# Gate weights turned by TensorE transposes instead of an element-wise copy, and a new order of scores and values in sigmoid attention ahead of two mixture layers

## The chip, the cores and the metric

The kernel runs on one core of one Trainium2 chip. The metric is the device time of one execution in microseconds. The kernel before was timed three times: 807.14, 807.19 and 807.71 us, a median of 807.19 us. Lower is better.

## What is computed

Three steps in fp32: attention with a sigmoid in place of the softmax (4 batches, 12 heads, 448 positions, head size 64), a layer that takes the larger of three projections and projects the result again, and a mixture of eight experts of which each token takes one.

```python
scores = scale * np.matmul(q, k.transpose(0, 1, 3, 2)) - np.log(S)
attn = 1.0 / (1.0 + np.exp(-scores))
x = np.matmul(attn, v)                      # -> [1792, 768]
h = np.maximum(np.maximum(x @ w1, x @ w2), x @ w3)
x = h @ w_out
logits = x @ w_gate + modality_bias[modality_id]     # w_gate is [768, 8]
e_idx = np.argmax(logits, axis=1)
...
for e in range(E):
    h = np.maximum(x[mask] @ w1[e], 0.0)
    out[mask] = gate_w[mask, None] * (h @ w2[e])
```

## The kernel before

The change lies in the first stage, attention. Its unit of work is a pair of heads of one batch: 24 units, numbered u, handled two at a time in a loop over j (A = 2j, B = 2j + 1). The 448 keys of a unit are three blocks of 128 and a rest of 64. For each unit there are four kinds of TensorE work:

- `emit_qk` (line 295): scores of the three full blocks of keys, six matmuls for each block, fp32r operands, rows 0 to 63 of the array for one head and 64 to 127 for the other. Query and key are first split by VectorE into a rounded part and a rest (`split_qk`, lines 275 and 276, into the tile `kq`, one buffer for even units and one for odd), and the product is made of three terms.
- `emit_qk_last` (line 310): scores of the last 64 keys of both units of a pair at once, four fp32 matmuls, one on each quarter of the array, straight from the loaded input.
- `emit_av` (line 320): attention times values over the three full blocks, six fp32 matmuls, columns 0 to 63 for one head and 64 to 127 for the other, into the PSUM tile `X` (tag `x0` for even units, `x1` for odd).
- `emit_av_last` (line 328): the same for the last 64 keys of both units, four fp32 matmuls on quarters of the array.

Each fp32 matmul shows in the trace as two records. Scores go into PSUM tiles `s` of which three exist (tags `a0`, `a1`, `t`); ScalarE takes the sigmoid from there (line 285), one instruction for each block and one for the last keys of a pair: seven for each pair of units. When the last keys are added, VectorE takes `X` out of PSUM (`evac_X`, lines 336 and 337).

The order on TensorE, ScalarE, VectorE and SyncE is the order in which the code is written; GpSimd is ordered by the framework. All loads of this stage are issued on SyncE, in that order, and each DMA there waits for the DMA issued eight before it. Inputs are loaded two pairs ahead: in pair j, after `emit_qk_last(j)`, units 2j + 4 and 2j + 5 (`load_qk`, line 254, into the tiles `u`; `load_v`, lines 260 to 265). The load of query and key waits for the scores that still read its buffer. In pair 4, after these loads, four small transfers stand on the same queue:

```python
nc.sync.dma_start(out=slots.rearrange("(p c) o -> p (c o)", p=128), in_=idx)
with nc.allow_non_contiguous_dma(reason="small"):
    nc.sync.dma_start(out=wgT, in_=w_gate.rearrange("d e -> e d"))
nc.sync.dma_start(out=mb, in_=m_bias.partition_broadcast(128))
nc.sync.dma_start(out=midi, in_=mid.bitcast(I32).rearrange("(i p t) -> p i t", p=128, t=2))
```

`wgT` is a scratch tensor in DRAM that holds the gate weights with the experts as rows; it is read in the second stage (line 436), one expert's row at a time, spread over the partitions. From pair 2 on, `background(2.5, ...)` gives VectorE some 2.5 us of another job in each pair: weights of the second stage, loaded as 64-bit numbers (`stage`, line 216), are turned into fp32 (lines 165 to 182). The second stage begins with the matmuls of line 457 as soon as the last `X` is out.

Of the kernel before, what the change touches and what calls it, by code (L numbers as in the profile page):

```python
# [28 lines left out]
def attn_moe_kernel(  # L29
# [15 lines left out]
    nc = tc.nc  # L45
    B, HP, D, _, _, S = qk.shape
    NT, DM = out.shape
    E, _, FF = ew1.shape
    KB = DM // 128
    FB = FF // 128  # L50
    NU = B * HP
# [23 lines left out]
    def hold(tag, name, *shape):  # L75
        return pool.tile([128, *shape], F32, tag=tag, name=name)

    def r(ap):
        return ap.bitcast(F32R)

    def cut(a, off, *shape):

        n = 1
        for s in shape:
            n *= s
        a = a[:, off:off + n]
        if len(shape) == 2:
            a = a.rearrange("p (a b) -> p a b", a=shape[0])
        elif len(shape) == 3:
            a = a.rearrange("p (a b c) -> p a b c", a=shape[0], b=shape[1])  # L90
        return a
# [10 lines left out]
    NW = 2 * NJ  # L102
# [5 lines left out]
    kq = [cut(kq_, 4 * S * i, 2, 2, S) for i in range(2)]  # L108
    u1, u2, u3 = (hold(f"U{i}", f"u{i}", 2048) for i in range(3))
    qk_in = [cut(u, 2 * S * i, 2, S) for u in (u1, u2) for i in range(2)]  # L110
    v4 = hold("K1", "v4", 2, NW + 1, D)
    v_in = [cut(u3, (NW + 1) * D * i, NW + 1, D) for i in range(4)] + [v4[:, i] for i in range(2)]

    stage = [hold(f"S{i}", f"stage{i}", KB * 256).bitcast(I32) for i in range(2)]
# [7 lines left out]
    wgT = dram.tile([E, DM], F32, name="wgT")  # L122
# [3 lines left out]
    ident = cpool.tile([128, 128], F32, name="ident")  # L126
# [21 lines left out]
    def ps(tag, shape, name):  # L148
        return psum.tile(shape, F32, tag=tag, name=name)
# [101 lines left out]
    def load_qk(u):  # L251
        b, hp = divmod(u, HP)
        for h in range(2):
            nc.sync.dma_start(out=qk_in[u % 4][D * h:D * (h + 1)], in_=qk[b, hp, :, h])  # L254
# [12 lines left out]
    def split_qk(u):  # L267
        src, kt = qk_in[u % 4], kq[u % 2]
        if u == 0:
            nc.vector.tensor_copy(out=r(kt[:, 0, 0]), in_=src[:, 0])  # L270
            nc.scalar.activation(out=r(kt[:, 0, 1]), in_=src[:, 1], func=ACTF.Copy)
            for i in range(2):
                nc.vector.tensor_tensor(out=r(kt[:, 1, i]), in0=src[:, i], in1=kt[:, 0, i], op=ALU.subtract)
        else:
            nc.vector.tensor_copy(out=r(kt[:, 0]), in_=src)  # L275
            nc.vector.tensor_tensor(out=r(kt[:, 1]), in0=src, in1=kt[:, 0], op=ALU.subtract)
# [3 lines left out]
    def scores():  # L280
        s_n[0] += 1
        return ps(("a0", "a1", "t")[s_n[0] % 3], [128, 2, 512], "s")

    def sigmoid(dst, s):
        nc.scalar.activation(out=dst, in_=s[:, :, 0:S], func=ACTF.Sigmoid, scale=qscale, bias=nlns)  # L285

    def emit_qk(u):

        kt = kq[u % 2]
        for g in range(NJ):  # L290
            s = scores()
            for n, (a, x) in enumerate(((0, 0), (0, 1), (1, 0))):
                for h in range(2):
                    p = slice(D * h, D * (h + 1))
                    nc.tensor.matmul(s[:, h, 0:S], r(kt[p, a, 0, 128 * g:128 * (g + 1)]), r(kt[p, x, 1]),  # L295
                                     start=(n == 0), stop=(n == 2))
            sigmoid(atb[u % 2][:, 2 * g:2 * g + 2], s)

    def quarter(i, h):

        return slice(SR * (h ^ i), SR * ((h ^ i) + 1))

    def emit_qk_last(j):

        s = scores()
        for i in range(2):
            src = qk_in[(2 * j + i) % 4]
            for h in range(2):
                p = slice(D * h, D * (h + 1))
                nc.tensor.matmul(s[quarter(i, h), i, 0:S], src[p, 0, 128 * NJ:], src[p, 1], start=True, stop=True)  # L310
        sigmoid(atl[j % 2], s)
# [3 lines left out]
    def emit_av(u):  # L315
        X_t[u] = ps(f"x{u % 2}", [128, 512], "X")
        vt, at = v_in[u % 6], atb[u % 2]
        for g in range(NJ):
            for h in range(2):
                nc.tensor.matmul(X_t[u][64 * h:64 * h + 64, 0:S], vt[:, 2 * g + h], at[:, 2 * g + h],  # L320
                                 start=(g == 0), stop=False)

    def emit_av_last(j):
        for i in range(2):
            u = 2 * j + i
            for h in range(2):
                p = quarter(i, h)
                nc.tensor.matmul(X_t[u][64 * h:64 * h + 64, 0:S], v_in[u % 6][p, NW], atl[j % 2][p, i],  # L328
                                 start=False, stop=True)

    def evac_X(u):
        b, hp = divmod(u, HP)
        src = X_t.pop(u)[:, 0:S]
        dR = xR[hp][:, b * S:(b + 1) * S]
        dL = xL[hp][:, b * S:(b + 1) * S]
        nc.vector.tensor_copy(out=r(dR), in_=src)
        nc.vector.tensor_tensor(out=r(dL), in0=src, in1=dR, op=ALU.subtract)

    with tc.manual_schedule(engines={mybir.EngineType.PE, mybir.EngineType.Activation, mybir.EngineType.DVE, SP}):
        load_qk(0)  # L340
        nc.vector.memset(gw, 0.0)
        nc.vector.memset(ones, 1.0)
        make_identity(nc, ident)
# [35 lines left out]
        for j in range(NU // 2 + 1):  # L379
            A, B, more = 2 * j, 2 * j + 1, j < NU // 2  # L380
            if more:
                emit_qk(A)
            if j:
                emit_av(B - 2)
                emit_av_last(j - 1)
                evac_X(A - 2)
                evac_X(B - 2)
            if not more:
                break
            emit_qk_last(j)  # L390
            for u in (A + 4, B + 4):
                if u < NU:
                    load_qk(u)
                    load_v(u)
            if A + 2 < NU:
                split_qk(A + 2)
            if j == 1:
                load_chunk()
            if j == 4:
                nc.sync.dma_start(out=slots.rearrange("(p c) o -> p (c o)", p=128), in_=idx)  # L400
                with nc.allow_non_contiguous_dma(reason="small"):
                    nc.sync.dma_start(out=wgT, in_=w_gate.rearrange("d e -> e d"))
                nc.sync.dma_start(out=mb, in_=m_bias.partition_broadcast(128))  # L403
                nc.sync.dma_start(out=midi, in_=mid.bitcast(I32).rearrange("(i p t) -> p i t", p=128, t=2))
            if j >= 2:
                background(2.5, stop=(1, 0))
            emit_qk(B)
            emit_av(A)
            if B + 2 < NU:
                split_qk(B + 2)  # L410
        background(99, stop=(1, 0))

        nc.vector.tensor_copy(out=midf, in_=midi[:, :, 0])
# [488 lines left out]
        for p, (i, n) in enumerate(todo[:NF * NCH]):  # L902
# [9 lines left out]
            else:  # L912
                f = n - 2 * KB
# [27 lines left out]
        d = xo[xo_n[0] % 3]  # L941
# [7 lines left out]
    with tc.For_i(NSTAT, nreg, 1) as iv:  # L949
        nc.sync.dma_start(out=idx2, in_=slots.rearrange("(p c) o -> p (c o)", p=128)[:, bass.ds(iv * 2, 2)])  # L950
        nc.sync.dma_start(out=e_dyn, in_=exd[0:1, bass.ds(iv, 1)])
        e = nc.values_load(e_dyn[0:1, 0:1], engines=(SP,), min_val=0, max_val=E - 1)
# [51 lines left out]
```

## Time and profile before

| | before |
|---|---|
| median of 3 runs | 807.19 us |
| the profiled execution | 807.75 us |
| its span, first to last instruction | 806.0 us |
| mean granted TensorE clock | 0.974 of 2.4 GHz |
| TensorE busy with matmuls | 760.3 us, 94% of the span |
| VectorE busy | 448.5 us, 56% |
| ScalarE busy | 258.6 us, 32% |
| attention, until the first matmul of line 457 | 168.63 us |

The profiled execution is one execution, 0.07% above the median. Its time is 1.75 us longer than its span, which is what lies around the first and the last instruction. Busy time of TensorE is the time covered by matmul records; TensorE works nearly the whole span, so what ends the kernel is read from the chain of waits: followed back from the last instruction, it is on TensorE for 87% of the span and on SyncE's DMA queue for 6%. In the chain, the waits and the timeline a line number is that of the kernel, `SPq` is SyncE issuing a DMA, and `out<-in` names the tiles. `PEclk` is the granted clock as a share of 2.4 GHz.

### The profile page before, as it was taken

The numbers are of one execution on the slowest core, as the hardware profiler recorded it, in microseconds if no ns is written. First come the engines' busy times: TensorE is split into PE (matmuls) and PEld (weight loads), VectorE is DVE, ScalarE is ACT, GpSimd is POOL, SyncE is SP. The second block draws the span as 40 slices with busy tenths as digits, with TensorE's granted clock in tenths as the row PEclk, the third lists the DMA queues.
The fourth block names the chain that finished last, engine by engine and source line by source line (L and its number), as shares of the span: only waits on it lengthen the run. The fifth ranks groups of instructions, "written<-read, shape, count | busy, mean of one in ns | idle before, by whom it ended". The sixth has DMA issues, their size and how long they took to land.

```text
span 806.0 us, 11821 instructions
## 1 busy us (share of the span) xinstructions
PE 760.3 (94%) x4698; PEld 642.0 (80%) x4698; DVE 448.5 (56%) x751; ACT 258.6 (32%) x362; POOL 65.2 (8%) x82
## 2 busy tenths in 40 slices
PE   9998059999999999999999999999999999999994
PEld 5454034479999999999997888998999999899993
DVE  3685047666696878784305822246665466555532
ACT  5665025520101010010003323245544445454522
POOL 0000000000000000000010060230220302021000
PEclk9999569999999999999999999999999999999998
DMA  8767596313242131220000196343657401064000
GB/s 206 206 148 2 3 225 164 109 40 118 77 153 83 59 117 59 79 79 1 0 1 1 54 368 243 102 144 133 249 171 263 157 22 59 14 246 148 20 25 18
DMA packets 50920, 88.04 MB, mean 109 GB/s; under 512 B 14219, under 2 KB 32908, under 8 KB 50862
## 3 DMA queue, kind: packets, MB, share of 16 engines
q1 hardware_dynamic: 47294, 75.71, 33.1%
q0 software_dynamic: 3568, 11.54, 4.3%
q8 instruction: 39, 0.64, 0.3%
q14 instruction: 19, 0.16, 0.1%
HBM read 94.95 MB, written 11.57 MB: 132 GB/s over the span
## 4 chain that ended last, share of the span: by engine, by line
PE 87%; SPq 6%; issue 2%; DMA 2%; DVE 1%; POOL 0%; ACT 0%; POOLq 0%; DVEq 0%
PE acc L457 33%; PE oacc L796 15%; PE hacc L775 14%; PE acc L523 7%; PE X L320 6%; PE s L295 5%; SPq L403 4%; PE acc2b L523 4%; DMA u<-in_qk_dram 2%; PE X L328 1%; PE xT L736 1%; PE s L310 1%; SPq L254 1%; PE lgp L483 1%; SPq L216 1%
## 5 line engine op out<-in xcount | busy, mean ns | idle before, releaser
L457 PE MATMUL acc<-xR,w_ring 128*128 128x448 f32 x864 | 210.5, 365 | 0.0
L457 PEld LDWEIGHTS acc<-xR,w_ring 128*128 128x128 f32 x864 | 162.2, 188 | 13.5 <-issue 0.7
L796 PE MATMUL oacc<-wo_ck,xh 128*128 128x512 f32 (+1 forms) x672 | 124.0, 340 | 0.0
L775 PE MATMUL hacc<-xh,wo_ck 128*128 128x256 f32 x1008 | 122.3, 283 | 0.0
L775 PEld LDWEIGHTS hacc<-xh,wo_ck 128*128 128x128 f32 x1008 | 121.9, 192 | 0.3
L796 PEld LDWEIGHTS oacc<-wo_ck,xh 128*128 128x128 f32 x672 | 102.8, 188 | 13.8
L285 ACT ACTIVATE at<-s,nlns 128x896 f32<-128x896 f32 x84 | 78.2, 1008 | 80.8 <-PE s L295 51.3
L457 PE MATMUL acc<-xLa,w_ring 128*128 128x448 f32 x360 | 102.2, 365 | 0.0
L295 PE MATMUL s<-kq 64*128 64x448 f32 x432 | 53.7, 388 | 31.8 <-DVE kq L275 31.2
L295 PEld LDWEIGHTS s<-kq 64*128 64x128 f32 x432 | 38.8, 190 | 54.2 <-issue 39.7
L182 DVE TENSOR_TENSOR wo_ck<-raw,wo_ck 128x512 fp32r<-128x512 f32 (+1 forms) x108 | 75.4, 743 | 6.0 <-ACT wo_ck L181 5.8
L523 PE MATMUL acc<-wo_ck,hs 128*128 128x512 f32 x252 | 77.4, 394 | 0.0
L457 PEld LDWEIGHTS acc<-xLa,w_ring 128*128 128x128 f32 x360 | 67.6, 188 | 5.3
L181 ACT ACTIVATE wo_ck<-raw 128x512 fp32r<-128x512 f32 (+1 forms) x108 | 67.0, 671 | 11.5 <-PE hacc L775 11.3
L523 PEld LDWEIGHTS acc<-wo_ck,hs 128*128 128x128 f32 x252 | 47.2, 188 | 11.4 <-ACT wo_ck L181 0.8
L523 PE MATMUL acc2b<-wo_ck,hs 128*128 128x256 f32 x252 | 56.2, 280 | 0.0
L439 DVE SCALAR_TENSOR_TENSOR gk<-wof,gk 128x768 f32<-128x768 f32 x48 | 45.9, 956 | 1.2
L461 ACT ACTIVATE hA<-acc 128x896 f32<-128x896 f32 x8 | 7.4, 920 | 115.1 <-PE acc L457 115.1
L782 DVE SCALAR_TENSOR_TENSOR xh<-hacc,xh 128x1024 fp32r<-128x1024 f32 x14 | 17.1, 1224 | 46.3 <-ACT xh L781 46.3
L727 POOL DMA_INDIRECT xg<-x2d,idx x30 | 30.0, 1000 | 148.2 <-PE xT L736 101.0
L523 PEld LDWEIGHTS acc2b<-wo_ck,hs 128*128 128x128 f32 x252 | 41.5, 189 | 0.1
L320 PE MATMUL X<-at,u 128*64 128x448 f32 x192 | 40.4, 557 | 0.0
(175 smaller groups left out, 666.5 us busy)
## 6 DMA issues: line engine op xcount, KB each, us to landing
raw<-in_moe_w_dram SPq DMA_DIRECT2D x24, 1024.0 KB
stage<-in_moe_w_dram SPq DMA_DIRECT2D x18, 768.0 KB
u<-in_qk_dram SPq DMA_DIRECT2D x48, 224.0 KB
raw<-in_moe_w_dram SPq DMA_DIRECT2D x12, 768.0 KB
raw_S<-in_moe_w_dram SPq DMA_DIRECT2D x12, 768.0 KB
stage<-in_moe_w_out_dram SPq DMA_DIRECT2D x6, 768.0 KB
x2d<-xo SPq DMA_DIRECT2D x14, 256.0 KB
gk<-wgT SPq DMA_DIRECT2D x8, 384.0 KB
```

The source lines that it names most:

```text
L181: nc.scalar.activation(out=r(dR), in_=src, func=ACTF.Copy)
L182: nc.vector.tensor_tensor(out=r(dL), in0=src, in1=dR, op=ALU.subtract)
L285: nc.scalar.activation(out=dst, in_=s[:, :, 0:S], func=ACTF.Sigmoid, scale=qscale, bias=nlns)
L295: nc.tensor.matmul(s[:, h, 0:S], r(kt[p, a, 0, 128 * g:128 * (g + 1)]), r(kt[p, x, 1]), start=(n == 0), stop=(n == 2))
L320: nc.tensor.matmul(X_t[u][64 * h:64 * h + 64, 0:S], vt[:, 2 * g + h], at[:, 2 * g + h], start=(g == 0), stop=False)
L403: nc.sync.dma_start(out=mb, in_=m_bias.partition_broadcast(128))
L439: nc.vector.scalar_tensor_tensor(out=junk, in0=wof[kb], scalar=1.0, in1=wgb[e % 2], op0=ALU.mult, op1=ALU.mult, accum_out=gw[:, kb, e:e + 1])
L457: nc.tensor.matmul(acc[:, c, 0:S], r(m[:, a, kk, :]), r(x[kk][:, c0 + S * c:c0 + S * (c + 1)]), start=(kk == 0 and n == 0), stop=(kk == KB ...
L523: nc.tensor.matmul(acc_t[t, c], r(hs[t][:, a, kk, :]), r(wo_rl[c][:, kk, b]), start=(kk == 0 and n == 0), stop=(kk == KB - 1 and n == 2))
L727: nc.gpsimd.indirect_dma_start(out=xg[i % 2][s][:, XC[c][0]:XC[c][1]], out_offset=None, in_=x2d[c], in_offset=bass.IndirectOffsetOnAxis(ap ...
L775: nc.tensor.matmul(acc[:, f], r(w[a][:, 128 * f:128 * (f + 1)]), r(x[:, kk]), start=(kk == 0 and m == 0 and f % 2 == 0), stop=(kk == KB - ...
L796: nc.tensor.matmul(dst, r(x[:, f, 128 * s:128 * (s + 1)]), r(w[a][:, c0:c1]), start=(f == 0 and m == 0 and not (shared and s == 1)), stop= ...
```

## The change

- The transfer into `wgT` on SyncE is gone. Instead GpSimd loads `w_gate` as it is, 128 partitions by 6 rows of 8 numbers, at the very start of the kernel, ahead of its other work, into a part of the tile that also holds two of the six value buffers (tag K1).
- In pair 0, between the scores of the last keys and the scores of unit B, six TensorE transposes turn it (`turn_gate`) into two PSUM tiles of tags `x0` and `x1`, VectorE copies them out, and GpSimd stores the turned weights to `wgT`.
- `emit_av(B)` moves from the next pair, where it stood after `emit_qk(A)`, to the end of its own pair, behind `emit_av(A)`. So the values of the two units stand in one run, and `emit_av_last(j - 1)` and `emit_qk_last(j)` stand between `emit_qk(A)` and `emit_qk(B)`.
- `split_qk(B + 2)` moves ahead of `background(2.5, ...)` and of the values.

```diff
-    v4 = hold("K1", "v4", 2, NW + 1, D)
+    k1 = hold("K1", "k1", 3 * DM)
+    v4 = cut(k1, 0, 2, NW + 1, D)
+    wg_in = cut(k1, 2 * (NW + 1) * D, KB, E)
+    wg_t = k1[0:E, 2 * DM:3 * DM]
...
+    def turn_gate():
+
+        for x, k0, k1 in ((0, 0, 4), (1, 4, KB)):
+            T = ps(f"x{x}", [128, 512], "wgp")
+            for k in range(k0, k1):
+                nc.tensor.transpose(T[0:E, 128 * (k - k0):128 * (k - k0 + 1)], wg_in[:, k], ident)
+            nc.vector.tensor_copy(out=wg_t[:, 128 * k0:128 * k1], in_=T[0:E, 0:128 * (k1 - k0)])
+        nc.gpsimd.dma_start(out=wgT, in_=wg_t)
...
         load_qk(0)
+        nc.gpsimd.dma_start(out=wg_in, in_=w_gate.rearrange("(k p) e -> p k e", p=128))
         nc.vector.memset(gw, 0.0)
...
             if more:
                 emit_qk(A)
             if j:
-                emit_av(B - 2)
                 emit_av_last(j - 1)
                 evac_X(A - 2)
                 evac_X(B - 2)
             if not more:
                 break
             emit_qk_last(j)
+            if not j:
+                turn_gate()
             for u in (A + 4, B + 4):
...
             if j == 4:
                 nc.sync.dma_start(out=slots.rearrange("(p c) o -> p (c o)", p=128), in_=idx)
-                with nc.allow_non_contiguous_dma(reason="small"):
-                    nc.sync.dma_start(out=wgT, in_=w_gate.rearrange("d e -> e d"))
                 nc.sync.dma_start(out=mb, in_=m_bias.partition_broadcast(128))
                 nc.sync.dma_start(out=midi, in_=mid.bitcast(I32).rearrange("(i p t) -> p i t", p=128, t=2))
+            emit_qk(B)
+            if B + 2 < NU:
+                split_qk(B + 2)
             if j >= 2:
                 background(2.5, stop=(1, 0))
-            emit_qk(B)
             emit_av(A)
-            if B + 2 < NU:
-                split_qk(B + 2)
+            emit_av(B)
         background(99, stop=(1, 0))
```

SyncE's queue in pair 4, from the last load of that pair (`v`) to the first of pair 5 (`qk`). `6144x1x1` is 6144 pieces of one number. Before:

```order
L265 DMA u_73<-in_v_dram 64x64 x2
L400 DMA slots<-idx 128x30
L402 DMA wgT<-in_moe_w_gate_dram 6144x1x1
L403 DMA mb<-in_moe_modality_bias_dram 128x16
L404 DMA midi<-in_moe_modality_id_dram 128x14x2
L216 DMA stage_75<-in_moe_w_dram 128x6x256
L254 DMA u_72<-in_qk_dram 64x896 x2
```

Changed:

```order
L268 DMA u_73<-in_v_dram 64x64 x2
L414 DMA slots<-idx 128x30
L415 DMA mb<-in_moe_modality_bias_dram 128x16
L416 DMA midi<-in_moe_modality_id_dram 128x14x2
L219 DMA stage_75<-in_moe_w_dram 128x6x256
L257 DMA u_72<-in_qk_dram 64x896 x2
```

One row has left; the transfer of the modality numbers (`midi`) and all that follows keep their places.

TensorE from the first scores to the scores of unit 3 (`s<-kq x18` is one unit's scores, `s<-u` the last keys' scores, `X<-at,u x6` one unit's values, `X<-at,u x4` the last keys' values). Before:

```order
L295 MATMUL s<-kq 128x448 x18
L310 MATMUL s<-u_71 64x448 x4
L295 MATMUL s<-kq 128x448 x18
L320 MATMUL X<-at,u_73 64x448 x6
L295 MATMUL s<-kq 128x448 x18
L320 MATMUL X<-at,u_73 64x448 x6
L328 MATMUL X<-at,u_73 64x448 x4
L310 MATMUL s<-u_72 64x448 x4
L295 MATMUL s<-kq 128x448 x18
```

Changed:

```order
L298 MATMUL s<-kq 128x448 x18
L313 MATMUL s<-u_71 64x448 x4
L339 MATMUL wgp<-ident,k_74 8x128 x6
L298 MATMUL s<-kq 128x448 x18
L323 MATMUL X<-at,u_73 64x448 x12
L298 MATMUL s<-kq 128x448 x18
L331 MATMUL X<-at,u_73 64x448 x4
L313 MATMUL s<-u_72 64x448 x4
L298 MATMUL s<-kq 128x448 x18
```

The six transposes (`wgp`) have come in, and the second run of six value matmuls has moved up to the first, so that the last keys' values and scores follow the scores of unit 2 directly.

## Rows read from the trace of the kernel before

**Rows 1.** The page: its span, and lines of the span in 40 equal slices (busy tenths of TensorE, its granted clock in tenths, busy tenths of the DMA engines).

```profile
span 806.0 us, 11821 instructions
PE   9998059999999999999999999999999999999994
PEclk9999569999999999999999999999999999999998
```

**Rows 2.** The chain of waits in order of time, one pair of units (start us, us, what).

```profile
35.83 2.02 PE s L295 x14
37.84 2.41 PE X L320 x12
40.25 0.91 PE X L328 x8
41.17 0.75 PE s L310 x8
41.92 2.09 PE s L295 x18
44.00 2.41 PE X L320 x12
```

**Rows 3.** The same chain at the end of attention.

```profile
163.06 4.66 PE X L320 x24
...
168.63 1.42 PE acc L457 x6
```

**Rows 4.** The same chain from 58.95 us on.

```profile
58.95 30.48 SPq L403
...
89.47 0.43 SPq L404
...
89.95 4.43 SPq L216
...
94.50 5.39 SPq L254
...
99.98 8.59 DMA u<-in_qk_dram
...
108.59 0.64 DVE kq L275
...
110.40 3.35 PE s L295 x16
113.76 3.24 PE X L320 x12
```

**Rows 5.** Waits between 70 and 115 us (engine, line, for whom: us in total, times, longest).

```profile
DVE kq L275 <- DMA u<-in_qk_dram: 33.2, 1, 33.2
...
PE s L295 <- DVE kq L275: 31.2, 1, 31.2
```

**Rows 6.** The timeline of 50 to 125 us (start us, us, engine, line; in brackets the idle time before and what ended it).

```profile
52.51 1.10 SPq L254 DMA_DIRECT2D u<-in_qk_dram  x2
52.64 3.71 ACT L285 ACTIVATE at<-s,nlns 128x896 f32<-128x896 f32 x4 [2.52 <-PE s L310]
...
58.09 0.81 SPq L402 DMA_DIRECT2D wgT<-in_moe_w_gate_dram  x1
...
109.37 0.74 PE L295 MATMUL s<-kq 64*128 64x448 f32 x2 [31.22 <-DVE kq L275]
```

**Rows 7.** Busy time in stretches: from:to, its length, busy us of TensorE (matmuls, weight loads), VectorE, ScalarE, GpSimd, each with its instructions, the granted clock, the busy share of the DMA engines, and GB/s.

```profile
59.00:78.00 19.00, 19.00 (x134) 8.71 (x134) 12.22 (x18) 11.90 (x13) 0.00 (x0) 1.00 0.72 10
...
89.40:94.40 5.00, 0.00 (x0) 0.00 (x0) 0.00 (x0) 0.00 (x0) 0.00 (x0) 0.50 0.15 1
...
108.60:114.00 5.40, 4.34 (x20) 3.11 (x22) 5.23 (x8) 2.15 (x3) 0.00 (x0) 0.50 1.07 216
114.00:168.60 54.60, 54.60 (x383) 25.47 (x379) 34.17 (x49) 30.61 (x33) 0.00 (x0) 0.99 0.50 132
```

**Rows 8.** The same view of the start.

```profile
3.00:4.00 1.00, 1.00 (x4) 1.00 (x4) 0.00 (x0) 0.00 (x0) 0.00 (x0) 1.00 1.08 308
```

**Rows 9.** The timeline of the start.

```profile
5.26 0.39 DVE L270 CAST kq<-u 128x448 fp32r<-128x448 f32 x1 [3.96 <-DMA u<-in_qk_dram]
...
7.62 6.40 ACT L285 ACTIVATE at<-s,nlns 128x896 f32<-128x896 f32 x7 [1.79 <-PE s L295]
...
9.63 2.63 PE L295 MATMUL s<-kq 64*128 64x448 f32 x18
```

**Rows 10.** The timeline at the first TensorE transposes of the third stage, 128 by 128, on TensorE.

```profile
524.44 1.04 PE L736 MATMUL xT<-ident,xg 128*128 128x128 f32 x8
525.23 1.32 PE L523 MATMUL acc2b<-wo_ck,hs 128*128 128x256 f32 x9
```

**Rows 11.** The instructions of line 746, a copy from PSUM (least, median and most ns, first and last start, form).

```profile
L746 DVE COPY ht<-hxT x3: 423/425/426, 762.4 to 771.3; 128x256 f32<-128x256 f32 x3
```

**Rows 12.** The timeline of GpSimd: an indirect DMA of 128 rows that it issues.

```profile
522.70 0.94 POOL L727 DMA_INDIRECT xg<-x2d,idx  x1 [0.30 <-issue]
```

**Rows 13.** DMA issues by line, with the size of one.

```profile
wgT<-in_moe_w_gate_dram SPq DMA_DIRECT2D x1, 24.0 KB
...
mb<-n_moe_modality_bias_dram SPq DMA_DIRECT2D x1, 8.0 KB
midi<-in_moe_modality_id_dram SPq DMA_DIRECT2D x1, 14.0 KB
```

## Prediction

> **What bounds the kernel now.** I read the slices of the page first. TensorE is busy nearly throughout but in the fourth to sixth (8, 0 and 5 tenths) and the last, and in the fifth and sixth the granted clock falls too [rows 1]. The stretches give the hole its size: no matmuls in 89.4 to 94.4 us, the DMA engines at 15% [rows 7]. The waits name it: TensorE stood 31.2 us for VectorE's split of a query and key, and VectorE 33.2 us for the load of it, unit 14's [rows 5]. The chain says why that load was late: SyncE stood 30.48 us in one instruction, the issue of `mb` [rows 4]. `mb` is 8 KB; the transfer right ahead of it, `wgT`, is 24 KB [rows 13] in 6144 pieces of one number. Its own issue took 0.81 us [rows 6], but in the time after it the DMA engines were 72% busy and moved 10 GB/s [rows 7], which is what many tiny pieces look like. I read it so: `wgT` fills the queue, and the next issue, whichever it is, waits until it has drained, 30.48 / 6144 = 5.0 ns for a piece.
>
> Everywhere else in attention TensorE sets the pace: a pair of units takes 2.02 + 2.41 + 0.91 + 0.75 + 2.09 + 2.41 = 10.59 us on it without a gap [rows 2], and from 114 us on it is busy throughout [rows 7]. So time taken out of TensorE's row there is time gained, and attention's end moves with it; the later stages follow in the same order and keep their lengths.
>
> **Part 1, the transfer that leaves SyncE.** TensorE's wait ended at 109.37 us after 31.22 us [rows 6], so it began at 78.15. When work came back the granted clock was 0.50, the lower level of 1.2 GHz, for a while [rows 7]: scores and values of the first unit end at 113.76 + 3.24 = 117.00 us [rows 4], 7.63 us after 109.37, and an ordinary pair of these takes 2.02 + 2.41 = 4.43 [rows 2]. The wait and the slow restart come to 31.2 + 3.2 = 34.4 us.
>
> What is late next? `midi` stays on the queue, and after it the loads of `stage` and of unit 14 stood 4.43 and 5.39 us [rows 4]; it is 14 KB for 1792 tokens, small pieces again. From its issue at 89.47 to unit 14's landing at 108.57 are 19.1 us [rows 4]. In the changed kernel that chain starts right after the loads of pair 4: they began at 52.51 and had let `wgT` through at 58.09 [rows 6], 5.6 us; with some 0.5 for `mb`, 19.1 and the first cast of 0.64 [rows 4], unit 14 is ready 25.8 us after the last keys' scores of pair 4. TensorE needs it at the start of pair 7. Before, that was 78.15 − 52.51 = 25.6 us later, so with the old order there would be nothing to spare. In the new order the last keys' scores end 2.02 + 0.91 + 0.75 = 3.68 us into a pair, so pair 7 begins 3 × 10.43 − 3.68 = 27.6 us after them. The reserve is 1.8 us. I put the rest of the stall at 0, with 4 us as the upper bound (nearly the 4.43 us of one held issue, if pair 4's own loads are still in the engines when `midi` starts).
>
> **Part 2, the new order in a pair.** Two units' values in a row took 4.66 us at the end of attention [rows 3], against 2 × 2.41 = 4.82 in pairs [rows 2]: 0.16 us less for one change of work saved. The last keys' values then follow scores and not values; I take the same 0.91 us, since values cost 2.41 after scores of either kind. 11 pairs gain: 11 × 0.16 = 1.8 us. The bounds are 0 and twice that. What could eat it is ScalarE: four sigmoids take 3.71 us [rows 6], so seven take 6.5 of 10.4 us. The scores now come within 5.8 us instead of spread over the pair, through three tiles. The tightest place is the last block of unit B, which needs the tile of the last keys' scores: written by 3.68 us, its sigmoid is done about 1.07 later (0.93 and a hand-over), at 4.75, and the block starts at about 5.1. It fits by 0.35 us; if not, what is lost is at most some tenths a pair. VectorE has both `X` out (two casts and two subtractions, about 2.5 us) before the values at 5.8 us want the tiles, and its conversions now stand behind both splits, so they delay neither.
>
> **Part 3, the turning of the gate weights.** Eight transposes 128 by 128 took 525.23 − 524.44 = 0.8 us [rows 10], so six take 0.6, and with a change of work 0.8. Unit 1's scores, before which they stand, took 2.63 us where 2.09 is normal [rows 9, 2], as ScalarE was the slower one there (seven sigmoids without a gap for 6.40 us [rows 9]). 0.5 us of the 0.8 falls into that, 0.3 us counts. The bounds are 0 and 2 us. The Trainium skill, "TensorEngine Tiling (Array Packing)", under "Gotcha 2: Feature Incompatibilities", says that column tiling rules out the transpose mode for fp32 input; were the eight-column output such a case, six plain fp32 products of 128 columns would take 2.41 / 3 × 128 / 448 × 6 = 1.4 us and the sum would be 0.8 us longer; no run here shows it yet. Two copies on VectorE, near 0.43 us each [rows 11], stand ahead of the split for unit 2, which has some 4 us to spare with both values ahead of unit 2's scores; they cost nothing. The store to `wgT` waits for nobody near and is read in the second stage.
>
> The load of `w_gate` is 768 pieces of 32 bytes. The trace has no such load from GpSimd. Bound below: GpSimd's DMA of 128 rows takes 0.94 us to issue [rows 12], and all is there long before the transposes at about 9.7 us. Bound above for the issue: six times 0.94 + 0.30, 7.4 us, which with a landing of two ends about where TensorE arrives. Beside that the pieces share the DMA engines with the first loads, which have them fully busy [rows 8]; at `wgT`'s price of 5.0 ns, 768 pieces are 3.8 us of all engines. The first split waits for such a load [rows 9], and all work behind it. I take 0.8 us, nearer to none, because the issue takes time and the first load is under way by then; the bounds are 0 and 3.8.
>
> **The sum**, against the profiled 807.75 us: 807.75 − 34.4 − 1.8 + 0.3 + 0.8 = 772.7. The profiled run is 0.56 above the median of 807.19, so I forecast 772.1 us, 4.3% less.
>
> **The rivals.**
> 1. The wait moves to `midi`. For it: its pieces held the queue for nearly 10 us, and the reserve is 1.8 us, by numbers from an otherwise empty queue. Against it: the new order starts the loads earlier in the pair. Up to 4 us more: 774 to 776.
> 2. The small reads delay the first loads. Up to 3.8 instead of 0.8: 775.1 us. The Trainium skill, "DMA: Bandwidth & Descriptors", "Rules for kernel authors", says that DMAs from SP, ACT and GpSimd all run on the same 16 engines and interleave, so that another queue saves only issue time; by it this rival is the full 3.0 us beyond my sum. The trace has the engines full there [rows 8] and can't say who yields.
> 3. The change doesn't do what it says: the 30 us belong to `mb`, whose row has them, and `mb` stays. Then only parts 2 and 3 are left: 807.2 − 1.8 + 1.1 = 806.5. Against it: 8 KB at 128 rows is no work for 30 us, and the tiny pieces are `wgT`'s.
> 4. Slower: `w_gate` lands late through GpSimd's queue, and six transposes stand at the head of TensorE's row with all of attention behind them. Each us after about 10 us costs a us; from 45 us on, 59 ns for each piece, the gain of 35 us is gone, and at 50 us the time is 812. The rows hold against it: 0.94 us for 128 rows is 7 ns a row.
>
> **How the numbers follow.** The forecast as summed (770 to 774) gets 0.66, rival 1 gets 0.15, rival 2 0.14, rival 3 0.03, rival 4 0.02. The range from 769.8 to 776.8 holds the first and nearly all of rivals 1 and 2: below, 1.8 us more from the order and 0.5 from the start; above, rival 1 or 2 in full. 0.2% is about what a measurement here can tell from no change, 1.6 us. Rival 3 (0.7 us gain) lies within it: faster 0.95, same 0.03, slower 0.02.
>
> **What would show it.** In the profile after: no fifth and sixth slice with a low clock, and attention ending near 133.5 us instead of 168.63. SyncE's `mb` issue under 1 us, `stage` and the load behind `midi` still held for 4 to 5 us each; if TensorE waits at pair 7 all the same, rival 1 is right. 4.66 us for two units' values in each pair and a period of 10.43; if 10.59 or more, part 2 is wrong, and a sigmoid will be what ended the wait. A first cast well behind 5.26 us tells rival 2, and a gap ahead of the transposes tells the price of the late load. If `mb` still holds the queue for 30 us, my reading of the hold is wrong.

## The result, and the profile after

| | before | after |
|---|---|---|
| median (lowest to highest, runs) | 807.16 us (806.36 to 807.71, 4) | 775.07 us (773.35 to 775.89, 4) |
| the profiled execution | 807.75 us | 775.12 us |
| its span | 806.0 us | 773.4 us |
| TensorE busy | 760.3 us, 94% | 757.6 us, 98% |
| attention, until the second stage's first matmul | 168.63 us | 134.95 us |
| from there to the end of the span | 637.37 us | 638.45 us |

The changed kernel takes 0.960 of the time before, with an interval of 0.9582 to 0.9618. It is 32 us faster and 3.0 us (0.4%) slower than the forecast of 772.1 us, inside the range of 769.8 to 776.8. Line numbers after are 3 to 14 higher than before.

The page of the changed kernel: span, busy tenths of TensorE in 40 slices, granted clock in tenths. These answer to [rows 1].

```profile
span 773.4 us, 11854 instructions
PE   8999999999999999999999999999999999999993
PEclk9999999999999999999999999999999999999997
```

The hole in the fourth to sixth slices is gone, and the low clock with it. What was forecast of SyncE's queue is read from its timeline after (start us, us, what). It answers to [rows 4, 6].

```profile
59.73 0.53 SPq L414 DMA_DIRECT2D slots<-idx  x1
60.31 0.47 SPq L415 DMA_DIRECT2D mb<-n_moe_modality_bias_dram  x1
60.82 0.43 SPq L416 DMA_DIRECT2D midi<-in_moe_modality_id_dram  x1
61.35 0.90 SPq L219 DMA_DIRECT2D stage<-in_moe_w_dram  x1
64.79 1.11 SPq L257 DMA_DIRECT2D u<-in_qk_dram  x2
```

The issue of `mb` takes 0.47 us in place of 30.48. The two issues behind `midi`, for which 4 to 5 us each had been forecast, take 0.90 and 1.11: `midi` holds nothing.

The chain of waits after, of one ordinary pair and of the end of attention, answers to [rows 2, 3].

```profile
40.26 2.01 PE s L298 x18
42.27 0.91 PE X L331 x8
43.18 0.75 PE s L313 x8
43.93 2.08 PE s L298 x18
46.01 4.66 PE X L323 x24
50.67 2.01 PE s L298 x18
...
129.38 4.66 PE X L323 x24
134.04 0.91 PE X L331 x8
134.95 15.20 PE acc L470 x74
```

A pair takes 50.67 − 40.26 = 10.41 us (10.59 before, 10.43 forecast), its two units' values 4.66 us in one run. From 14.73 us on the chain stays on TensorE until attention ends; nothing waits at pair 7.

The start of the chain after (against [rows 9]):

```profile
1.46 4.70 DMA u<-in_qk_dram
...
6.26 0.41 DVE kq L273
...
6.69 1.17 DVE kq L276 x2
...
7.90 3.12 PE s L298 x15
11.02 0.92 PE s L313 x8
11.93 0.75 PE wgp L339 x6
12.69 2.05 PE s L298 x18
14.73 4.66 PE X L323 x24
```

The first cast starts at 6.26 us instead of 5.26, and the scores behind it take 3.12 us. The transposes (`wgp`) take 0.75 us and wait for no DMA. The same chain of the kernel before has 1.89 us for its first 16 scores and begins its first values at 12.27 us:

```profile
6.91 1.89 PE s L295 x16
...
12.27 2.40 PE X L320 x12
```

In the timeline of the changed kernel's start, brackets hold the idle time ahead and what ended it:

```profile
1.38 1.02 POOL L353 DMA_DIRECT2D k<-in_moe_w_gate_dram  x1 [0.85 <-POOLq L1002]
...
6.88 0.74 PE L298 MATMUL s<-kq 64*128 64x448 f32 x2 [0.69 <-ACT kq L274]
```

GpSimd issued the 768 pieces in 1.02 us, far from the 7.4 us of the upper bound. They run beside the first loads, and TensorE stood 0.69 us ahead of the first scores, which it didn't before.

### The profile page after: what moved, and what is told of

It is laid out like the page before. It is cut to its first block, busy times and chain, and to the rows that moved or that the text cites. A ratio compares the mean times of both kernels' runs of the same rounds, so it can differ in the third digit from the quotient of the medians.

```text
span 773.4 us, 11854 instructions
## 1 busy us (share of the span) xinstructions
PE 757.6 (98%) x4704; PEld 643.3 (83%) x4704; DVE 449.1 (58%) x753; ACT 258.6 (33%) x362; POOL 67.5 (9%) x84
## 4 chain that ended last, share of the span: by engine, by line
PE 94%; issue 2%; DMA 2%; DVE 0%; POOL 0%; ACT 0%; SPq 0%; POOLq 0%; DVEq 0%
PE acc L470 34%; PE oacc L809 15%; PE hacc L788 15%; PE acc L536 8%; PE X L323 7%; PE s L298 6%; PE acc2b L536 4%; PE X L331 1%; PE s L313 1%; PE xT L749 1%; PE lgp L496 1%; DMA xg<-x2d,idx 1%; DMA u<-in_qk_dram 1%; DMA x2d<-xo 0%; PE hacc L941 0%
## 5 line engine op out<-in xcount | busy, mean ns | idle before, releaser
L788 PEld LDWEIGHTS hacc<-xh,wo_ck 128*128 128x128 f32 x1008 | 121.9, 192 | 0.3
L476 DVE TENSOR_TENSOR hB<-hB,acc 128x896 f32<-128x896 f32 x8 | 8.7, 1087 | 50.2 <-PE acc L470 50.2
```

Of the source, the lines that this page charges most:

```text
L788: nc.tensor.matmul(acc[:, f], r(w[a][:, 128 * f:128 * (f + 1)]), r(x[:, kk]), start=(kk == 0 and m == 0 and f % 2 == 0), stop=(kk == KB - ...
```

## The experiments

Kernels are compared within their batch, each of which had its own runs of the kernel before, since those medians differ (811.08, 816.37 and 815.23 us). The first theory: the hold of 30 us belongs to `wgT` and falls on whatever is issued next; the new order is worth 0.16 us a pair; what was lost against the forecast lies at the start. Its rivals: the hold belongs to `mb`; `midi` is a second holder; the price of the start is something other than the 768 pieces.

| batch | kernel | median us (range, runs) | ratio to before, 95% |
|---|---|---|---|
| 1 | the changed kernel again | 773.11 (772.83 to 774.85, 5) | 0.9542 (0.9519 to 0.9565) |
| 1 | turning alone, old order | 774.55 (774.26 to 775.08, 5) | 0.9557 (0.9535 to 0.9579) |
| 1 | one more warming round | 772.87 (772.54 to 774.94, 5) | 0.9545 (0.9521 to 0.9569) |
| 1 | gate weights read by rows | 772.89 (772.48 to 775.25, 5) | 0.9541 (0.9517 to 0.9565) |
| 2 | order alone, `wgT` kept | 813.2 (811.12 to 814.42, 7) | 0.9959 (0.9939 to 0.9979) |
| 2 | `wgT` behind `mb` and `midi` | 815.71 (814.95 to 817.19, 10) | 1.0003 (0.9988 to 1.0018) |
| 2 | half of the experts in pieces | 812.44 (811.12 to 813.28, 10) | 0.9954 (0.9939 to 0.9968) |
| 2 | rows and one more warming round | 779.03 (778.76 to 781.73, 5) | 0.9558 (0.9533 to 0.9584) |
| 3 | the changed kernel a third time | 778.51 (777.75 to 779.62, 5) | 0.9551 (0.9527 to 0.9575) |
| 3 | half of the depths in pieces | 796.98 (796.37 to 797.94, 4) | 0.9781 (0.9753 to 0.9810) |
| 3 | `midi` five pairs later | 815.25 (812.21 to 818.62, 10) | 1.0000 (0.9982 to 1.0018) |
| 3 | transposes ahead of the first scores | 777.41 (775.85 to 777.47, 5) | 0.9533 (0.9509 to 0.9557) |

**The changed kernel again**, beside the first batch, unedited:

> The changed kernel once more, so that the next three have it beside them on the same chip. 775.1 us as before. In the start: first cast at 6.26 us, first unit's scores 3.1 us. At the first gathers of the mixture stage TensorE waits for the transposed gather; 5.15 us from issue to landing if the 1.1 us that the later stages lost come back every time, 4.6 us or less if they were chance.

Measured 773.11 us, 0.9542. Its runs lie in two groups, 772.8 to 773.1 and 774.5 to 774.9; the profiled run is one of the upper. In it the first cast came at 5.65 us and the first scores took 3.10 us, slow once more. The gather of the mixture stage for which the expectation named 5.15 us or 4.6 and less took 4.71 us, between the two.

**Turning alone**, the old order of scores and values put back:

```diff
+                emit_av(B - 2)
                 emit_av_last(j - 1)
...
-            emit_qk(B)
-            if B + 2 < NU:
-                split_qk(B + 2)
             if j >= 2:
                 background(2.5, stop=(1, 0))
+            emit_qk(B)
             emit_av(A)
-            emit_av(B)
+            if B + 2 < NU:
+                split_qk(B + 2)
```

> The turning of the gate weights of the changed kernel with the old order of scores and values. Theory: the order is worth 11 times 0.16 us and nothing else, the hold on the queue is all the transfer's: 776.9 us, and no wait at pair 7, since the transfer of the modality numbers holds nothing by itself. Rival (that of the prediction): that transfer holds the queue 10 us, the old order leaves it no reserve, and TensorE waits for unit 14, some 2 to 4 us: 779 to 781 us.

It is 1.44 us slower than the changed kernel; beside a kernel with an equally fast start (the rows, below) its attention ends 1.7 us later, 134.8 against 133.1. So the order is worth about what was forecast (1.8), and the rest of the gain is the turning's. The rival of `midi` falls: here the old order, which had nothing to spare by the prediction, ran without a wait at pair 7. SyncE's timeline of this kernel:

```profile
59.87 0.43 SPq L417 DMA_DIRECT2D midi<-in_moe_modality_id_dram  x1
60.95 0.88 SPq L219 DMA_DIRECT2D stage<-in_moe_w_dram  x1
63.67 1.11 SPq L257 DMA_DIRECT2D u<-in_qk_dram  x2
```

**Order alone**, the transfer into `wgT` kept: on the kernel before.

```diff
             if j:
-                emit_av(B - 2)
                 emit_av_last(j - 1)
...
-            if j >= 2:
-                background(2.5, stop=(1, 0))
             emit_qk(B)
-            emit_av(A)
             if B + 2 < NU:
                 split_qk(B + 2)
+            if j >= 2:
+                background(2.5, stop=(1, 0))
+            emit_av(A)
+            emit_av(B)
```

> The kernel before with the new order of scores and values alone; the gate weights still go element by element on SyncE's queue. Theory: the hold of 30.5 us stays, but it begins earlier, as the loads of pair 4 are let through 2.4 us earlier in the pair and four pairs ahead of it are 0.16 us shorter each, and the pairs behind it gain 0.16 us each: 807.2 less 2.4, less 11 times 0.16, about 803 us. Rival: the order gains its 0.16 us a pair and no more, since the wait starts earlier too: 805.4 us.

It gains 3.2 us, with an interval from 1.7 to 5.0 that holds both expectations. The hold of `mb` stays, and TensorE's wait at pair 7 is 32.0 us:

```profile
58.52 31.64 SPq L402 DMA_DIRECT2D mb<-n_moe_modality_bias_dram  x1
```

So the order alone removes none of the stall, whatever it lets through earlier.

**`wgT` last of the three**, on the kernel before:

```diff
-                with nc.allow_non_contiguous_dma(reason="small"):
-                    nc.sync.dma_start(out=wgT, in_=w_gate.rearrange("d e -> e d"))
                 nc.sync.dma_start(out=mb, in_=m_bias.partition_broadcast(128))
                 nc.sync.dma_start(out=midi, in_=mid.bitcast(I32).rearrange("(i p t) -> p i t", p=128, t=2))
+                with nc.allow_non_contiguous_dma(reason="small"):
+                    nc.sync.dma_start(out=wgT, in_=w_gate.rearrange("d e -> e d"))
```

> The kernel before with the two other small transfers (modality bias and modality numbers) moved ahead of the element-wise one. Theory: the hold is the element-wise transfer's, and falls on whatever is issued behind it: the bias and the numbers are issued in about 1 us each, and the load of the second stage's weights behind now takes about 30 us. The 10 us that the two loads after the modality numbers were held are gone, if they came from those numbers queued behind the pieces, which would make it some 797 us; if the pieces themselves hold a second time, 807 us. Rival: the bias holds the queue by itself, 30 us, ahead of the element-wise transfer.

SyncE's timeline:

```profile
59.25 0.44 SPq L401 DMA_DIRECT2D mb<-n_moe_modality_bias_dram  x1
59.73 0.44 SPq L402 DMA_DIRECT2D midi<-in_moe_modality_id_dram  x1
60.21 0.81 SPq L404 DMA_DIRECT2D wgT<-in_moe_w_gate_dram  x1
61.08 32.87 SPq L216 DMA_DIRECT2D stage<-in_moe_w_dram  x1
94.06 1.14 SPq L254 DMA_DIRECT2D u<-in_qk_dram  x2
```

`mb` and `midi` pass in 0.44 us each, and the 32.87 us fall on the next issue behind `wgT`, now that of `stage`. That shows whose the hold is, and that the row which carries it only stands next. The total is unchanged (1.0003), which the expectation had put down to pieces that hold a second time. Unit 14's load was issued right behind the hold with no `midi` between, and still it took 16.48 us to land (the chain):

```profile
94.67 16.48 DMA u<-in_qk_dram
```

**Half of the experts in pieces**, the other half as a plain copy of the same size:

```diff
+                nc.sync.dma_start(out=wgT[4:8], in_=w_gate.rearrange("(a b) e -> a (b e)", a=8)[4:8])
...
-                    nc.sync.dma_start(out=wgT, in_=w_gate.rearrange("d e -> e d"))
+                    nc.sync.dma_start(out=wgT[0:4], in_=w_gate[:, 0:4].rearrange("d e -> e d"))
```

> The kernel before with four experts' gate weights turned element by element (3072 pieces) and the other four rows of the scratch filled by a plain copy, so that half of the gate weights are not the right ones. Theory: the hold goes by the piece, 5.0 ns each: the bias is held 15 us and the time falls by 15 to 792 us. Rival: the queue takes some thousands of pieces before it holds anything, so that the hold falls by more than half, to some us, and the time to 782 us or less.

Both theories missed: with 3072 pieces instead of 6144 `mb` is still held for 28.15 us, and the gain is 3.9 us. The stretches of this kernel (columns as in [rows 7]; the share of the DMA engines is the last but one):

```profile
74.00:78.00 4.00, 4.00 (x30) 2.05 (x28) 1.53 (x3) 3.66 (x4) 0.00 (x0) 1.00 0.44 0
...
86.00:90.00 4.00, 0.00 (x0) 0.00 (x0) 0.00 (x0) 0.00 (x0) 0.00 (x0) 0.50 0.42 0
```

In these two stretches the engines are 44 and 42% busy; from 66 to 90 us it is 41 to 62% in steps of 4 us, where it is 87 to 98% with all eight experts (the run with `midi` later, below). I read that so: half of the engines have as many pieces as before and the others none, as an expert's 768 pieces lie behind each other on the same engines. The trace's records of single pieces, which no view lists, bear out the half: between 62.7 and 92 us at most nine pieces are under way at once in this run, and 16 or 17 for 38% of that time in the kernel before. Then the price is not per piece of the transfer but per piece of an engine's share, which the next run tests.

**Half of the depths in pieces**, all eight experts, the other half again as a plain copy, to test that:

```diff
+                nc.sync.dma_start(out=wgT[:, 384:768], in_=w_gate[384:768].rearrange("(a b) e -> a (b e)", a=8))
...
-                    nc.sync.dma_start(out=wgT, in_=w_gate.rearrange("d e -> e d"))
+                    nc.sync.dma_start(out=wgT[:, 0:384], in_=w_gate[0:384].rearrange("d e -> e d"))
```

> The kernel before with half of the gate weights turned element by element in the other direction: all eight experts, the first 384 of 768 depths, 3072 pieces; the other halves are filled by a plain copy, so that half of the gate weights are not the right ones. With four whole experts the hold had stayed at 28 us while the DMA engines' busy share fell to half, so the pieces of one expert seem to lie one behind the other on the same engines. Theory: here every engine keeps its share and has half the pieces; busy share as in the kernel before (0.95), hold near 15 us, time some 15 us less than before. Rival: the hold is a fixed price of such a transfer: 28 to 30 us again, and the time level with before.

The same 3072 pieces, now over all engines (102% in 62 to 66 us): `mb` is held for 12.83 us, TensorE waits 15.9 us instead of 31.2, and 18.3 us are gained. The chain of this kernel:

```profile
59.85 12.83 SPq L404
...
82.18 11.09 DMA u<-in_qk_dram
...
95.17 3.36 PE s L295 x16
```

**`midi` five pairs later**, on the kernel before, to see who holds the 10 us behind `mb`:

```diff
+            if j == 9:
+                nc.sync.dma_start(out=midi, in_=mid.bitcast(I32).rearrange("(i p t) -> p i t", p=128, t=2))
...
-                nc.sync.dma_start(out=midi, in_=mid.bitcast(I32).rearrange("(i p t) -> p i t", p=128, t=2))
```

> The kernel before with the modality numbers loaded in pair 9 instead of right behind the element-wise transfer and the bias. Theory: after the 30 us the two loads stood another 10 us, with the DMA engines at 0.1 to 0.4, because the numbers' pieces run on few engines; without them there the loads follow at once, and the time falls by some 10 us against before, with no new wait in pair 9 (in the changed kernel the numbers hold nothing). Rival: the 10 us are the rest of the element-wise transfer and stay: level with before.

The time is unchanged (1.0000). `stage` is issued right behind the hold in 0.43 us, but the load of unit 14 is held all the same, now for 7.72 us, and lands 12.90 us later (the chain):

```profile
58.82 31.55 SPq L405
...
90.41 0.43 SPq L216
...
90.96 7.72 SPq L254
...
98.78 12.90 DMA u<-in_qk_dram
```

With no `midi` on the queue the second hold is there; with no `wgT` on it (the changed kernel, the turning alone) it isn't. So it comes with `wgT`. The waits of SyncE name `wgT` as what a later load waited for (`SPq L263`, 2.1 us, until about 103.6 us), 45 us after its issue. The stretches show how busy the DMA engines are meanwhile:

```profile
82.00:86.00 4.00, 0.00 (x0) 0.00 (x0) 0.00 (x0) 0.00 (x0) 0.00 (x0) 0.50 0.98 1
86.00:90.00 4.00, 0.00 (x0) 0.00 (x0) 0.00 (x0) 0.00 (x0) 0.00 (x0) 0.50 0.87 1
90.00:94.00 4.00, 0.00 (x0) 0.00 (x0) 0.00 (x0) 0.00 (x0) 0.00 (x0) 0.50 0.24 0
94.00:98.00 4.00, 0.00 (x0) 0.00 (x0) 0.00 (x0) 0.00 (x0) 0.00 (x0) 0.50 0.03 1
```

They are full until about 89 us, and from 94 to 98 they are 3% busy while the issue stands. By the records of single pieces the stream of 4-byte pieces ends at 92.0 us but for some 40 until 95.2 (all by 91.6 in the kernel before), and up to 98 us there is then hardly more than the 64-byte pieces of `mb`, a few at a time. So what holds the issue last is not pieces in work; what is awaited stays open.

**One more warming round**, for the slow first scores:

```diff
-    WARM = 7
+    WARM = 8
```

> The changed kernel with one more warming matmul at the start (8 for 7). Theory: the first load lands 1.0 us later than in the kernel before, TensorE stands 0.69 us, and its clock then stays low through the first unit's scores (574 ns a matmul for 362), which costs 1.2 us more; with the gap filled the scores take 1.9 us, and the time falls by 1.2 to 773.9 us. Rival: the gap has nothing to do with it and the scores stay at 3.1 us: 775.1 us.

In the profiled run the first cast came at 5.67 us, as late as in the changed kernel beside it (5.65), and TensorE stood 0.60 us ahead of the first scores instead of 0.99. The scores were at full speed (the chain):

```profile
7.31 1.89 PE s L298 x16
```

Its attention ended at 133.1 us against 134.7. But the medians are level, 772.87 and 773.11 us, and the runs of both fall into the same two groups. So in one trace the gap is shorter, not filled, and the scores are fast, as they also are with seven rounds in the two other edited kernels of the batch (1.89 and 1.91 us); no gain of the round was measured.

**Gate weights read by rows**, 128 pieces of 192 bytes instead of 768 of 32, and copies that put the order right:

```diff
-            nc.vector.tensor_copy(out=wg_t[:, 128 * k0:128 * k1], in_=T[0:E, 0:128 * (k1 - k0)])
+            nc.vector.tensor_copy(out=wg_t.rearrange("e (p k) -> e k p", k=KB)[:, k0:k1],
+                                  in_=T[0:E, 0:128 * (k1 - k0)].rearrange("e (k p) -> e k p", p=128))
...
-        nc.gpsimd.dma_start(out=wg_in, in_=w_gate.rearrange("(k p) e -> p k e", p=128))
+        nc.gpsimd.dma_start(out=wg_in, in_=w_gate.rearrange("(p k) e -> p k e", k=KB))
```

> The changed kernel with the gate weights read as 128 rows of 192 bytes instead of 768 pieces of 32, and written out of PSUM with a stride to make up for it. Theory: the 768 small pieces delay the first load of query and key by 1.0 us; with 128 the first cast is back near 5.3 us, the first unit's scores at 1.9 us, and the time falls by 2.2 to 772.9 us. Rival: any DMA beside the first loads costs about the same, whatever its pieces: first cast at 6.2 us, 775 us.

GpSimd's issue took 0.73 us (1.02), yet the first cast came at 5.62 us, beside 5.58 to 5.67 in the three kernels of the batch with 768 pieces:

```profile
5.62 0.39 DVE L273 CAST kq<-u 128x448 fp32r<-128x448 f32 x1 [4.32 <-DMA u<-in_qk_dram]
```

So the number of pieces isn't what makes the first load late in these runs. The first scores took 1.89 us, and the median is level with the changed kernel.

**Both small edits together**, the two diffs above in one kernel:

```diff
-    WARM = 7
+    WARM = 8
...
-        nc.gpsimd.dma_start(out=wg_in, in_=w_gate.rearrange("(k p) e -> p k e", p=128))
+        nc.gpsimd.dma_start(out=wg_in, in_=w_gate.rearrange("(p k) e -> p k e", k=KB))
```

> The changed kernel with both of the small edits, the gate weights read as 128 rows and eight warming matmuls. Each alone was level with the changed kernel within 0.3 us, with the first unit's scores at 1.9 us in the profiled run of both. If the slow scores come in some of the executions and the two make them rarer, 772.7 us with a smaller spread than the 2 us of the changed kernel; if not, the same 773 us with the same spread.

First cast at 5.51 us, first scores 1.88 us, a ratio of 0.9558 to the kernel before on its chip: no gain beside the changed kernel's three ratios (0.960, 0.9542, 0.9551), and with 3.0 us between its fastest and slowest run no smaller spread.

**The changed kernel a third time**, beside the last edit:

> The changed kernel once more, for the other three on the same chip: 773 to 775 us where the kernel before has 807, with first scores of 1.9 or 3.1 us from one execution to the next.

The latest first cast of all, 7.08 us, with TensorE standing 1.51 us ahead of the first scores, and these the slowest, 3.35 us for 16.

**Transposes ahead of the first scores**: the load by rows, and the six transposes between the warming matmuls and the first scores, where TensorE waits for the first split anyway. The copies follow the split of unit 1.

```diff
         split_qk(0)
+        turn_gate()
         split_qk(1)
+        store_gate()
...
             emit_qk_last(j)
-            if not j:
-                turn_gate()
```

> The changed kernel with the gate weights read as 128 rows and the six transposes put between the warming matmuls and the first scores, where TensorE waits for the first split; VectorE's copies follow the second split. Theory: the transposes' 0.75 us leave TensorE's full row, and the gap ahead of the first scores is filled, so attention ends 0.75 us earlier than in the changed kernel with fast first scores: 772.3 us if the changed kernel has 773.1 on the chip. Rival: the gate weights have not landed when the warming ends at 6.2 us, and the first scores wait for them: the gain is lost or turned round, by 1 us or more.

The timeline of TensorE in this kernel:

```profile
5.20 0.82 PE L341 MATMUL wgp<-ident,k 128*8 128x128 f32 x6
6.11 0.47 PE L298 MATMUL s<-kq 64*128 64x448 f32 x2
7.14 1.89 PE L298 MATMUL s<-kq 64*128 64x448 f32 x16 [0.55 <-DVE kq L276]
```

The transposes fill the wait. The first two records of scores follow them at once, the other 16, after 0.55 us in which TensorE waits for the split, at full speed, and attention ends at 132.7 us (137.0 in the changed kernel beside it, whose first cast came so late). Against the run by rows, whose start was fast, attention ends 0.4 us earlier (133.1), where 0.75 had been expected: unit 1's scores take 2.62 us again instead of 2.05. The time is 777.41 us against 778.51; the ranges (775.85 to 777.47 and 777.75 to 779.62) don't meet. So this version was 1.1 us (0.14%) faster than the changed kernel in this batch; how much of that is the place of the transposes and how much the changed kernel's late first load isn't told apart.

## Why the prediction was right, and where it was off

The prediction's parts 1 and 2 can be read in one sum, from the first values to the end of attention: the first values began at 12.27 us before (unit 1's scores of [rows 9] end there, 9.63 + 2.63) and at 14.73 after, attention ended at 168.63 and 134.95, so 156.4 us became 120.2: 36.1 us gained, 36.2 forecast.

**Part 1, the stall: right in size, wrong in half of its reading.** There is no wait at pair 7 and no low clock behind it; of the 36.1 us the order has 11 × 0.18 = 2.0, which leaves 34.1 for the stall, 34.4 forecast. The run with the turning alone gives it directly: from its first values at 12.85 us to the end of attention at 134.78 are 121.9 us, 34.4 less than before. That the hold was `wgT`'s was argued from its tiny pieces and is now shown: it goes where `wgT` goes (32.87 us on `stage`) and shrinks with its pieces (12.83 us). "5.0 ns for a piece" holds only over all engines; with the same pieces on half of them the hold stays (28.15 us). The Trainium skill, "DMA: Bandwidth & Descriptors", "Rules for kernel authors", says that an outermost dimension of fewer than 16 confines a transfer to at most that many engines. The runs agree that the number of rows outermost, as the code writes them, bears on how many engines work, but not on the number: eight rows had the 16 engines up to 98% busy, four rows 41 to 62%, and by that rule it would be at most half and a quarter.

**The step on `midi` failed.** "Its pieces held the queue for nearly 10 us", said the prediction, and it made of that a chain of 19.1 us and a reserve of 1.8. In the changed kernel `midi` holds nothing, and with `midi` moved away the second hold stayed. The 10 us came with `wgT`: quiet engines at 89.4 to 94.4 us [rows 7] were taken for an empty queue. `midi` was itself held up: by the records of single pieces its 1792 pieces ran for 4.3 us in the kernel before (95.9 to 100.2 us) and for 1.6 in the changed one (62.6 to 64.2). The result didn't depend on this step, since the forecast put the rest of the stall at 0; the 0.15 of rival 1 rested on it.

**Part 2, the order: right.** 0.18 us a pair instead of 0.16, 2.0 us instead of 1.8; 1.44 us by medians and 1.7 by two traces, put against the turning alone. The tight place at ScalarE cost nothing: the chain of the pairs has no piece but TensorE's.

**Part 3, the start: the mis-sized term.** The first values came 2.46 us later than before; 1.1 us had been forecast (0.3 and 0.8). The transposes were sized right: they took 0.75 us, and unit 1's scores 2.05, by the removed wait for ScalarE some 0.6 less than the 2.63 of [rows 9]. In the run by rows, whose start was fast, the first values came 7.24 us behind the first cast; before, 7.01. That is 0.23 us for 0.3. The prediction's sentence on column tiling had 1.4 us for them; with 0.75 that case isn't here, or costs nothing. What was too small is "I take 0.8 us" for the contention: the first cast came 1.0 us later, and behind it came a second price that the prediction had not seen. TensorE ran out of warming matmuls and stood, and the first scores then took 3.12 us for 1.89, some 1.2 us; the last section has a lower clock for them. Rival 2's 775.1 us was met, but by luck: it had up to 3.0 us more for the delayed load, and the load was 1.0 us late; the slow scores and the later stages made up the rest. Of its mechanism half is right: the load beside the first ones comes with a later first cast (5.58 us in the run with the turning alone, 5.24 in that with the order alone), but 128 pieces do so about as much as 768.

**What is left of the miss** in the profiled run is later: from the second stage on it took 638.45 us, before 637.37. Most of it lies at one gather of the mixture stage: from the end of the transfer ahead of it to the first products behind it are 6.74 us, before 5.96. This looks like chance. With the same instructions in that stage the same stretch took 6.43 us in the changed kernel's second run and 5.84 with one more warming round. And in the third batch the time from the second stage on is 640.9 and 642.8 us in the two profiled kernels that have the change, and 642.0 and 642.4 in the two that haven't. Span by span: 806.0 − 36.1 + 2.5 + 1.1 = 773.4 (rounded), against 806.0 − 36.2 + 1.1 = 770.9. The other 0.5 of the 3.0 us is the step from the profiled run to the median: the forecast took off 0.56, and the changed kernel's profiled run lies 0.05 above its median.

**The other rivals.** Rival 3 is out: `mb` took 0.47 us. Rival 4 is out: the issue took 1.02 us and the transposes waited for nothing. The other two batches gave ratios of 0.9542 and 0.9551, below the forecast's 772.1 / 807.19 = 0.9565, where the first gave 0.960: the forecast's size lies among the three.

## What to carry to other kernels

A transfer of single numbers is paid by whoever comes next on its queue, so look at the row ahead of the one that carries the wait, and ask how its pieces lie on the engines, not only how many there are (3072 held the next issue for 28.15 or 12.83 us); that the engines are quiet doesn't mean that the queue is free. An early small load on another queue wasn't free here while the first load is what everybody waits for; work that needs no input of the main path, as these transposes, can go into that first wait, where it also keeps TensorE busy. Where an edit takes away one long wait, what is late next is best tested by taking the suspect away, as with `midi`, before a price is put on it.

## What the runs showed that was not expected

- 6144 pieces of 4 bytes held the next issue for 30.5 to 32.9 us and the queue for some 10 us more, in part with engines 3% busy; half of the pieces held it for 28.15 us when they were of half of the experts, and 12.83 us when they were of half of the depths.
- A load of 24 KB on GpSimd's queue, issued in 0.73 to 1.02 us, came with a first cast at 5.50 to 7.08 us in the kernels that have it, and at 5.12 to 5.41 in the profiled runs of the six kernels without it. Above 5.67 us it was twice, both in unedited runs of the changed kernel; what sets it is open.
- Behind a gap of 0.69 to 1.51 us after the warming matmuls, the first 16 scores took 3.10 to 3.35 us in all three profiled runs of the changed kernel, as long as the 3.35 us at a granted clock of 0.50 (1.2 GHz) behind the long wait [rows 4, 7]. The gap came from a late load (first cast at 6.26 and 7.08 us) or, in the second run, from warming matmuls that were done in 3.94 us instead of 4.85. In that second run the column of the granted clock shows the lower level:

```profile
8.00:11.00 3.00, 3.00 (x18) 1.91 (x18) 1.53 (x2) 2.59 (x3) 0.00 (x0) 0.50 1.07 252
```

  In the first run the same stretch reads 1.00 (2.4 GHz), though its matmuls are as slow. The stretch, and line 298 up to 12 us (least, median and most ns):

```profile
8.00:11.00 3.00, 3.00 (x20) 2.45 (x20) 1.53 (x2) 1.83 (x2) 0.00 (x0) 1.00 1.07 253
```

```profile
L298 PE MATMUL s<-kq x18: 359/574/739, 6.9 to 10.7; 64*128 64x448 f32 x18
```

  There the trace's own records of the clock begin only at 10.62 us (at 14.22 in the third run, at 4.21 in the second, with the fall to 0.50 at 7.63), and the view counts the time ahead of the first record as full speed. So a 1.00 at the very start is to be held against the durations. With the transposes in the gap, the median of the same line is 362 ns. In the one run with a gap and fast scores (0.60 us), there was one more round of warming ahead of it.
